# The last batch's low-rank step moved one slot earlier and done over four PSUM banks

## The chip, the cores and the metric

The kernel runs on one core of one Trainium2 chip. The metric is the device time of one execution in microseconds; the time before is 290.36 us, the median of three runs (290.25 to 290.58). TensorE is called PE below, VectorE DVE, ScalarE ACT, GpSimd POOL, and SyncE (which here only issues DMAs) SP.

## The reference

Eight batches of linear ("cosformer") attention, with 8 heads, 576 positions and head size 64, are followed by a low-rank mix over the positions and a two-layer network over the 512 channels:

```python
q_p, k_p = phi(q), phi(k)              # relu(x)*cos, relu(x)*sin -> 128 features
kv  = einsum('bhsf,bhsd->bhfd', k_p, v)
z   = sum(k_p, axis=2)
x   = einsum('bhsf,bhfd->bhsd', q_p, kv) / (einsum('bhsf,bhf->bhs', q_p, z)[..., None] + 1e-6)
x   = x.transpose(0, 2, 1, 3).reshape(B, 576, 512)
h   = x.transpose(0, 2, 1) @ U @ V     # U: 576 x 32, V: 32 x 576
u   = x + h.transpose(0, 2, 1)
out = u + maximum(u @ w_ch1, 0) @ w_ch2   # 512 -> 2048 -> 512
```

## The kernel before, in words

The 576 positions of a batch are four blocks of 128 and a rest of 64. The rests ("tails") of two batches share one block of 128 rows, so there are four pairs of tails.

For each batch attention gives x. `A_unit` then makes A = Uᵀx (32 x 512), kept as four groups of 32 rows, one for each quarter j of the channels. `u_mm` multiplies V by A: for a position block c and a channel quarter j there is one product of 32 x 128 by 32 x 128 (line 476), 16 in all, and the four j use four different groups of 32 rows of PE and four different PSUM banks. `u_add` adds x to one bank on DVE (line 484, one instruction of 128 x 512 for each j). `u_tail` does the same for a pair of tails: eight small products (line 498), then one DVE add of 128 x 128 for each j (line 505). `utr_dma` transposes u by DMA on SP's queue (lines 522 and 528); the result uT feeds the first matmul of the network.

The program is an order written out by hand. `slots` is a list of functions that mostly issue PE work; `todo` holds what is issued right after a slot. Each engine takes its own instructions in that order. Around the change the slots alternate between two kinds, and counting `slots` in the code gives these numbers:

- Even slots 200 to 214 are `half_part`: eight products of 128 x 256 (`h_ps`, line 894) of batch 5's second matmul, then one addition on DVE ("more", line 850) or a copy on ACT.
- Odd slots 201 to 215 are the first matmul of batch 6, which is worked out for a pair of hidden blocks p with seven products of half size instead of eight. `g1_cross(b, p, i)`, i from 1 to 7, issues two matmuls of 128 x 256 (`c_ps`, line 677). `g1_join` takes the results apart: ACT copies P1, U2 and P5 (line 130), DVE adds C11, C22 and C12 (line 612), ReLUs R22, R21 (ACT, line 689) and one on DVE after C12 (line 699).

For a p the crosses write three places, X and Y in one bank (`g0` or `g1`, by p's parity) and Z in bank `T`. Cross 5 opens Z and cross 3 adds to it; Z is free again when C12 has read it. Cross 4 adds to X, which C22 must have read before.

| slot | what it issues before the change |
|---|---|
| 200 | h_ps; first sum for batch 5 (`hid_sum`, line 836) |
| 201 | cross 6 of p=4, U2; then `A_unit(7)` |
| 202 | h_ps; second sum |
| 203 | crosses 1, 2 of p=5 with P1, C11; cross 5 of p=4 with P5; cross 7 of p=4 with C22, R22; then `u_mm` of j = 0, 1, 2 and `u_add` 0 |
| 204 | h_ps, more; `u_add` 1; transposing DMA of the first half of u; fourth sum |
| 205 | crosses 3, 4 of p=4 with R21, C12; cross 6 of p=5; third sum |
| 206 | h_ps; then `u_mm` of j = 3 |
| 207 | as 203, for p=6 and p=5; then `u_add` 2 |
| 208 | h_ps; `u_add` 3; transposing DMA of the second half |
| 209 | as 205, for p=5 and p=6; a weight sum (`w1_sum`, line 612) |
| 210 | h_ps, more; `u_tail` of j = 0, 1, 2 |
| 211 | as 203, for p=7 and p=6 |
| 212 | h_ps, more; `u_tail` of j = 3; transposing DMA of the tails |
| 213 | as 205, for p=6 and p=7 |
| 214 to 217 | the rest of p=7, a tail block, and four sums of batch 7's uT (`uT_sum`, line 612) |

`u_mm` and `u_tail` take PSUM through `four_banks`: the two banks of X (the tag `"X"`, another thing than the cross's X) and then what is passed in: `("s", 1)` is bank `g2`, and `T1` is bank `T`, the one that holds Z. A bank is handed on when all that read its old content have ended.

The lines that the change touches or its steps name are 440 to 507 (`A_unit`, `four_banks`, `u_mm`, `u_add`, `u_tail`), 519 to 528 (`utr_dma`), 650 to 710 (crosses and joins), and 1051 to 1083 in `attention_plan`; batch 7 has w = 187 and a_at = 14.

Of the kernel before, what the change touches and what calls it, by code (L numbers as in the profile page):

```python
# [17 lines left out]
def kernel(  # L18
# [13 lines left out]
    B = 8  # L32
# [14 lines left out]
    def tail(b):  # L47
        lo = TS * (b % 2)
        return slice(lo, lo + TS)
# [390 lines left out]
    def A_of(b):  # L440
        return A_sb[b % 4]
# [27 lines left out]
    def u_mm(b, *spare, js=range(4)):  # L469
        if b not in u_bf:  # L470
            u_bf[b] = pool.tile([P, 4, 4, P], BF16, tag="u_bf", bufs=3, name="u_bf")
        va.setdefault(b, {}).update(zip(js, four_banks(*spare)))
        for c in range(4):
            for j in js:
                rows = slice(j * R, j * R + R)
                nc.tensor.matmul(  # L476
                    out=va[b][j][:, c * P : c * P + P], lhsT=V_bf[rows, c, :],
                    rhs=A_of(b)[rows, :], start=(c == 0), stop=(c == 3),
                    tile_position=(j * R, 0),
                )  # L480
# [5 lines left out]
            in1=va[b][j].rearrange("p (c n) -> p c n", c=4), op=ALU.add,  # L486
        )

    def u_tail(pr, *spare, js=range(4)):
        if pr not in u_tl:  # L490
            u_tl[pr] = pool.tile(
                [P, DM], BF16, tag="k_p" if pr == 3 else "u_tl", bufs=1, name="u_tl"
            )
        vt = dict(zip(js, four_banks(*spare)))
        for i in range(2):
            for j in js:
                rows = slice(j * R, j * R + R)
                nc.tensor.matmul(
                    out=vt[j][tail(i), 0:P], lhsT=V_tl[rows, :],
                    rhs=A_of(2 * pr + i)[rows, :], start=True, stop=True,  # L500
                    tile_position=(j * R, i * TS),
                )
        for j in js:
            ns = slice(j * P, j * P + P)
            nc.vector.tensor_tensor(
                out=u_tl[pr][:, ns], in0=x_tl[:, ns], in1=vt[j][:, 0:P], op=ALU.add
            )
# [144 lines left out]
    def g1_cross(b, p, i):  # L652

        if (b, p) not in cross:
            if b not in hid:
                hid[b] = pool.tile([P, NJ, 512], BF16, tag="hid", bufs=2, name="hid")
            of_x, of_z = CROSS[p % 2] if b == B - 1 else (("g0", "g1")[p % 2], "T")
            xy = psum.tile([P, 512], FP32, tag=of_x, bufs=1, name="c_ps")  # L660
            cross[b, p] = {"X": xy[:, 0:256], "Y": xy[:, 256:512], "of_z": of_z}
        w = cross[b, p]
        if i == 5:
            z = psum.tile([P, 512], FP32, tag=w["of_z"], bufs=1, name="c_ps")
            w["Z"] = z[:, 0:256]
        cs = slice(p * P, p * P + P)
        to, lhs, rhs, first = {
            1: lambda: ("X", W1[0], uT_quarter(b, 0, 0), True),
            2: lambda: ("Y", W1[1], uT_quarter(b, 1, 0), False),
            3: lambda: ("Z", w1_s[4], uT_quarter(b, 1, 1), False),  # L670
            4: lambda: ("X", W1[3], uT_s[b, 4], False),
            5: lambda: ("Z", w1_s[1], uT_s[b, 1], True),
            6: lambda: ("X", w1_s[2], uT_s[b, 2], False),
            7: lambda: ("X", w1_s[3], uT_s[b, 3], False),
        }[i]()
        for d in range(2):
            nc.tensor.matmul(  # L677
                out=w[to].rearrange("p (c t) -> p c t", c=2), lhsT=lhs[:, d, cs],
                rhs=rhs[:, d], start=(first and d == 0), stop=(d == 1),
                skip_group_check=not first,  # L680
            )
# [325 lines left out]
    def attention_plan(b):  # L1007

        plan = []
        if b < 4:  # L1010
            w, f_at, q_eng, k_eng, qtr, lo = PLAN[b]
        else:
            w, q_at, k_at, qtr, lo = PLAN[b]

        def put(at, f, *a, tag=False):
            if tag:
                a = a + spare(w + at)
            plan.append((w + at, lambda: f(b, *a)))

        for n, c in enumerate(QORD):  # L1020
            if b > 3:
                put(q_at[0] + q_at[1] * n, q_prep, c, q_at[2:])
                put(k_at[0] + k_at[1] * n, k_prep, c, k_at[2:])
                put(k_at[0] + (3 * n) // 2, v_prep, 0, H, (c,), (G_,))
                continue
            if b == 3:
                q_eng, k_eng = V_ if n == 3 else A_, A_ if n < 3 else None
                put((-15, -14, -13, -2, -6)[n], q_prep, c, (q_eng, q_eng))
                put(n - 12 if n < 3 else -8, k_prep, c, (A_, k_eng))
                if n > 2:  # L1030
                    put(-4, k_prep, c, (None, V_))
                put((-9, -9, -9, -7, -5)[n], v_prep, 0, H, (c,), (A_ if n > 2 else G_,))
                continue
            put(f_at + ((n - 1) % 5 if b == 2 else n), q_prep, c, (q_eng, q_eng))
            put(f_at + 6 + n, k_prep, c, (k_eng, k_eng))
            put((-5, -2, -1, -5, -5)[n], v_prep, 0, H, (c,), (V_ if n > 2 else A_,))
        for n, (c0, c1) in enumerate(((4, 5), (0, 2), (2, 4))):
            at = qtr[n] if b > 4 else -2 if b == 3 and n == 2 else qtr + 2 * n
            put(at, qtr_dma, c0, c1)
        plan.append((w + (b == 2), lambda: kv_unit(b, 0, *spare(w), A_)))  # L1040
        plan.append((w + 2, lambda: kv_unit(b, 1, *(T1 if b == 3 else spare(w + 2)), A_)))
        for n, c in enumerate(ORD):
            if b > 3:
                put((3 if b == B - 1 else 4) + 2 * n, x_unit, c, "X", 1)
            else:
                at = 4 + n if b == 3 else 4 + (3 * n) // 2
                if n % 2:
                    put(at, x_two, c, tag=True)
                else:
                    put(at, x_unit, c, "X", 1)  # L1050
        a_at = (12, 10)[b - 2] if b < 4 else 14
        if b == B - 1:
            put(a_at, A_unit, "s", 1, A_)
        else:
            put(a_at, A_unit, tag=True)
        odd = b % 2 == 1


        def two(at):
            return [T1, ("s", 1) if at >= 86 else G3] if at >= 86 or at < 64 else [spare(at)] * 2  # L1060

        if b == B - 1:
            plan.append((w + a_at + 2, lambda: u_mm(b, ("s", 1), js=(0, 1, 2))))
            plan.append((w + a_at + 5, lambda: u_mm(b, js=(3,))))
        else:
            u_at = w + a_at + (1 if b == 3 else 2)
            plan.append((u_at, lambda: u_mm(b, *two(u_at))))
        for j in range(4):
            n = (j + 1) // 2 if b == 2 else j // 2 - 1 if b == 3 else j + (2 if b > 4 and j > 1 else 0)
            put(a_at + 2 + n, u_add, j)  # L1070
        put(a_at + (2 if b == 3 else 3), utr_dma, 0, 2)
        put(a_at + (7 if b > 4 else 3 if b == 3 else 5), utr_dma, 2, 4)
        if odd:
            if b == B - 1:
                plan.append((w + a_at + 9, lambda: u_tail(b // 2, ("s", 1), js=(0, 1, 2))))
                plan.append((w + a_at + 11, lambda: u_tail(b // 2, js=(3,))))
            else:
                at = w + a_at + (10 if b == 5 else 8 if b == 3 else 9)
                plan.append((at, lambda at=at: u_tail(b // 2, *two(at))))
            put(a_at + (11 if b > 4 else 9 if b == 3 else 10), utr_dma, 4, 5)  # L1080
        for at, t in zip(lo, loads(b + 1) if lo else ()):
            plan.append((w + at, t))
        return plan
# [44 lines left out]
    T1 = ("T", 1)  # L1128
# [221 lines left out]
    def put(at, thunk):  # L1350
        todo.setdefault(at, []).append(thunk)
# [66 lines left out]
    b6, b7 = B - 2, B - 1  # L1418
# [11 lines left out]
    def fifth(b, p):  # L1430
        g1_cross(b, p, 5)
        g1_join(b, p, "P5")

    def third(b, p):
        g1_cross(b, p, 7)
        g1_join(b, p, "C22")
        g1_join(b, p, "R22")

    def closed(b, p):
        g1_cross(b, p, 3)  # L1440
        g1_cross(b, p, 4)
        g1_join(b, p, "R21")
        g1_join(b, p, "C12")

    def crossed(*steps):
        def go():
            for f, b, p in steps:
                f(b, p)

        return go  # L1450
# [19 lines left out]
    units = [g1(b6, j) for p in range(3) for j in (p, p + 8)] + [g1(b6, 3)]  # L1470
    units.append(lambda: [opened(b6, 4), g1_main(b6, 11)])
    units.append(crossed((sixth, b6, 4)))
    for p in range(5, 8):
        units.append(crossed((opened, b6, p), (fifth, b6, p - 1), (third, b6, p - 1)))
        units.append(crossed((closed, b6, p - 1), (sixth, b6, p)))
    units.append(crossed((fifth, b6, 7), (third, b6, 7)))
    slots += units[0:2]
# [128 lines left out]
```

## Time and profile before

| | |
|---|---|
| median of the runs | 290.36 us (290.25 to 290.58) |
| the profiled execution's own time | 290.29 us |
| its span from first to last instruction | 288.5 us |
| busy: PE | 281.9 us, 98% |
| busy: DVE | 212.0 us, 73% |
| busy: ACT | 169.2 us, 59% |
| busy: POOL | 64.7 us, 22% |
| mean granted PE clock | 0.999 |
| DMA | 56.17 MB |

The span is the part that the trace covers; 1.8 us of the execution lie around it. The chain that ended last is followed back from the last instruction to what released each step. Matmuls are pipelined: one of 128 x 256 is shown as 0.27 us long, but the next starts 0.109 us later. So PE's time is read from starts, and the same holds in part for DVE and ACT. In a timeline row the columns are the start, the length of the run of equal instructions, engine, line, operation, output and inputs, shapes and count; brackets give the engine's idle time before it and what ended it.

### The profile page before, as it was taken

How to read it: one execution, taken by the hardware profiler on the slowest of the kernel's cores; microseconds unless marked ns; L12 is line 12 of the kernel's file. 1: busy time of each engine (PE TensorE's matmuls, PEld its weight loads, DVE VectorE, ACT ScalarE, POOL GpSimd, SP SyncE). 2: the span in 40 equal slices, each digit the busy share in tenths (PEclk: the TensorE clock that was granted, in tenths of full speed). 3: DMA queues.
4: the chain of work that ended last, by engine and by line, in shares of the span. 5: the costliest groups of instructions: out<-in, count | busy, mean ns of one | idle time of the engine just before them, and what ended most of it. 6: DMA issues, size and time to landing. Idle time of an engine off the chain costs nothing.

```text
span 288.5 us, 7416 instructions
## 1 busy us (share of the span) xinstructions
PE 281.9 (98%) x2961; PEld 199.0 (69%) x2992; DVE 212.0 (73%) x515; ACT 169.2 (59%) x347; POOL 64.7 (22%) x98
## 2 busy tenths in 40 slices
PE   8999999999999999999999999999999999999995
PEld 4785564446788546776766666766777889889884
DVE  5977858896876888557547794669968787775763
ACT  2955752177893557577735964497644556657310
POOL 6520500000046103302400501024201313303330
PEclk9999999999999999999999999999999999999999
DMA  7999999999999999998699939993930754436113
GB/s 225 306 254 250 278 160 192 225 328 220 363 252 202 272 248 256 203 332 207 175 227 268 245 74 250 180 339 91 183 77 9 140 120 82 88 96 112 39 75 143
DMA packets 92933, 56.17 MB, mean 195 GB/s; under 512 B 56580, under 2 KB 89732, under 8 KB 92900
## 3 DMA queue, kind: packets, MB, share of 16 engines
q1 hardware_dynamic: 82020, 43.41, 60.5%
q0 software_dynamic: 10688, 12.09, 20.7%
q8 instruction: 23, 0.38, 0.5%
q10 hardware_dynamic: 192, 0.20, 0.2%
q14 instruction: 10, 0.08, 0.1%
HBM read 36.86 MB, written 9.44 MB: 160 GB/s over the span
## 4 chain that ended last, share of the span: by engine, by line
PE 85%; DMA 8%; DVE 2%; ACT 2%; issue 1%; DVEq 0%; ACTq 0%
PE h_ps L894 32%; PE g_ps L580 26%; PE c_ps L677 7%; DMA kst<-in_k_dram 6%; PE o_ps L762 6%; PE gt_ps L722 5%; PE kv_ps L348 3%; PE x_ps L423 3%; DMA qst<-in_q_dram 2%; PE h_ps L762 1%; PE a_ps L446 1%; PE va_ps L476 1%; DVE k_p L309 1%; ACT q_p L307 1%; DVE v_ext L132 1%
## 5 line engine op out<-in xcount | busy, mean ns | idle before, releaser
L580 PE MATMUL g_ps<-uT,w_bf 128*128 128x512 bf16 x378 | 95.5, 379 | 1.1
L589 ACT ACTIVATE hid<-g_ps 128x512 bf16<-128x512 f32 x104 | 61.4, 597 | 59.7 <-PE g_ps L580 57.2
L580 PEld LDWEIGHTS <-w_bf 128*128 128x128 bf16 x402 | 37.5, 98 | 33.7
L894 PEld LDWEIGHTS <-hid 128*128 128x128 bf16 x560 | 53.0, 98 | 10.7
L894 PE MATMUL h_ps<-w_bf,hid 128*128 128x256 bf16 x336 | 43.1, 273 | 0.1
L894 PE MATMUL h_ps<-w_s,S 128*128 128x256 bf16 x240 | 30.4, 273 | 0.0
L894 PE MATMUL h_ps<-w_s,hid 128*128 128x256 bf16 x224 | 29.0, 273 | 0.0
L850 DVE TENSOR_TENSOR o_sb<-o_sb,h_ps 128x256 f32<-128x256 f32 (+1 forms) x38 | 16.9, 446 | 13.7 <-PE h_ps L894 11.2
L953 POOL DMA_DIRECT2D out_dram<-o_sb x20 | 12.9, 646 | 60.8 <-DVE o_sb L850 48.3
L894 PEld LDWEIGHTS <-S 128*128 128x128 bf16 x240 | 23.1, 98 | 4.9
L850 DVE TENSOR_TENSOR o_sb<-u_bf,h_ps 128x256 f32<-128x256 bf16 x32 | 13.3, 416 | 14.8 <-PE h_ps L894 14.6
L132 POOL CAST v_ext<-vst 128x512 bf16<-128x512 f32 (+1 forms) x22 | 16.0, 755 | 33.1 <-DMA vst<-in_v_dram 29.8
L484 DVE TENSOR_TENSOR u_bf<-x_bf,va_ps 128x512 bf16<-128x512 bf16 x27 | 17.6, 680 | 5.2 <-PE va_ps L476 4.1
L612 DVE TENSOR_TENSOR hid<-kept,c_ps 128x256 bf16<-128x256 f32 x36 | 14.7, 417 | 8.3 <-ACT kept L130 4.6
L952 POOL DMA_DIRECT2D o_sb<-u_bf x8 | 10.4, 1301 | 32.4 <-DVE rec L414 15.5
L130 ACT ACTIVATE kept<-c_ps 128x256 f32<-128x256 f32 x36 | 12.6, 384 | 7.2 <-PE c_ps L677 7.2
L722 PE MATMUL gt_ps<-uT_tl,w_bf 128*128 128x128 bf16 x256 | 16.2, 219 | 0.0
L433 DVE TENSOR_TENSOR x_bf<-x_ps,rec 128x512 bf16<-128x512 f32 x22 | 15.2, 692 | 0.8
L722 PEld LDWEIGHTS <-w_bf 128*128 128x128 bf16 x256 | 15.1, 98 | 0.7
L762 PE MATMUL o_ps<-w_bf,hid 128*128 128x512 bf16 x61 | 14.6, 379 | 0.3 <-issue 0.2
L130 ACT ACTIVATE o_sb<-h_ps 128x256 f32<-128x256 f32 x24 | 9.2, 381 | 9.4 <-PE h_ps L894 8.7
L307 ACT ACTIVATE k_p<-kst,cosw 128x512 bf16<-128x512 f32 x20 | 14.2, 713 | 0.1
(189 smaller groups left out, 459.5 us busy)
## 6 DMA issues: line engine op xcount, KB each, us to landing
qst<-in_q_dram SPq DMA_DIRECT2D x14, 512.0 KB, 5.8
kst<-in_k_dram SPq DMA_DIRECT2D x12, 512.0 KB, 7.4
out_dram<-o_sb POOLq DMA_DIRECT2D x21, 256.0 KB, 3.8
vst<-in_v_dram SPq DMA_DIRECT2D x10, 512.0 KB, 8.0
w_bf<-in_moe_w_ch_dram POOLq DMA_DIRECT2D x7, 512.0 KB, 13.3
out_dram<-o_sb SPq DMA_DIRECT2D x14, 256.0 KB, 2.4
kst<-in_k_dram SPq DMA_DIRECT2D x4, 640.0 KB, 7.0
o_sb<-u_bf POOLq DMA_DIRECT2D x8, 256.0 KB, 3.8
```

Of the source, the lines that this page charges most:

```text
L130: nc.scalar.activation(out=o, in_=i, func=AF.Copy, bias=0.0, scale=1.0)
L132: eng.tensor_copy(out=o, in_=i)
L307: nc.scalar.activation(out=o, in_=i, func=AF.Relu, bias=0.0, scale=w)
L433: nc.vector.tensor_tensor(out=x_of(b, c, rows).rearrange("p (g i d) -> p g i d", g=2, d=D), in0=view[:, :, :, 0:D], in1=rec[rows].unsqueez ...
L484: nc.vector.tensor_tensor(out=u_bf[b][:, j, :, :], in0=x_bf[b][:, :, ns], in1=va[b][j].rearrange("p (c n) -> p c n", c=4), op=ALU.add,)
L580: nc.tensor.matmul(out=g_ps.rearrange("p (c t) -> p c t", c=4), lhsT=w1_bf[:, d, j * P : j * P + P], rhs=uT[b][:, d, :, :], start=(d == 0) ...
L589: nc.scalar.activation(out=hid[b][:, j, :], in_=g_ps, func=AF.Relu, bias=0.0, scale=1.0)
L677: nc.tensor.matmul(out=w[to].rearrange("p (c t) -> p c t", c=2), lhsT=lhs[:, d, cs], rhs=rhs[:, d], start=(first and d == 0), stop=(d == 1 ...
L722: nc.tensor.matmul(out=g_ps[:, jj, :], lhsT=w1_bf[:, d, j * P : j * P + P], rhs=uT_tl[pr][:, d, :], start=(d == 0), stop=(d == 3),)
L762: nc.tensor.matmul(out=o[:, cols], lhsT=lhs[:, j, c * P : c * P + P], rhs=w2_bf[:, j, cols], start=(j == 0), stop=(j == NJ - 1),)
L850: eng.tensor_tensor(out=o, in0=x, in1=y, op=ALU.add)
L894: nc.tensor.matmul(out=acc, lhsT=lhs[:, j, :], rhs=rhs[:, j, :], start=(j == 0 and at is not None), stop=(j == 7), skip_group_check=at is ...
```

## The change

For the last batch, `A_unit` comes a slot sooner (200 in place of 201). Its u is one `u_mm` of 16 products over four banks in slot 202, the fourth bank being T, which holds j = 0; before it was 12 products in slot 203 and 4 in slot 206. All offsets of batch 7 that follow from `a_at` move by one slot, though their lines are not edited: `u_add` 0 to 3 go from slots 203, 204, 207, 208 to 202, 203, 206, 207, and the transposing DMAs of u from 204 and 208 to 203 and 207. `u_tail` of the last pair is one step of eight products in slot 210 (before six there and two in slot 212); its third bank is T, which holds j = 2, and its adds run in the order 2, 3, 0, 1. The tails' transposing DMA stays in slot 212. In slot 203 cross 7 of p=4 is issued ahead of cross 5, which writes T.

```diff
-    def u_tail(pr, *spare, js=range(4)):
+    def u_tail(pr, *spare, js=range(4), first=0):
...
-        for j in js:
+        for j in (*js[first:], *js[:first]):
...
-        a_at = (12, 10)[b - 2] if b < 4 else 14
+        a_at = (12, 10)[b - 2] if b < 4 else 13 if b == B - 1 else 14
...
         if b == B - 1:
-            plan.append((w + a_at + 2, lambda: u_mm(b, ("s", 1), js=(0, 1, 2))))
-            plan.append((w + a_at + 5, lambda: u_mm(b, js=(3,))))
+            plan.append((w + a_at + 2, lambda: u_mm(b, T1, ("s", 1), js=(1, 2, 0, 3))))
...
             if b == B - 1:
-                plan.append((w + a_at + 9, lambda: u_tail(b // 2, ("s", 1), js=(0, 1, 2))))
-                plan.append((w + a_at + 11, lambda: u_tail(b // 2, js=(3,))))
+                plan.append((w + a_at + 10, lambda: u_tail(b // 2, T1, ("s", 1), first=2)))
...
-            put(a_at + (11 if b > 4 else 9 if b == 3 else 10), utr_dma, 4, 5)
+            put(a_at + (12 if b == B - 1 else 11 if b == 5 else 9), utr_dma, 4, 5)
...
+    def seventh_first(b, p):
+        g1_cross(b, p, 7)
+        fifth(b, p)
+        g1_join(b, p, "C22")
+        g1_join(b, p, "R22")
...
     for p in range(5, 8):
-        units.append(crossed((opened, b6, p), (fifth, b6, p - 1), (third, b6, p - 1)))
+        if p == 5:
+            units.append(crossed((opened, b6, p), (seventh_first, b6, p - 1)))
+        else:
+            units.append(crossed((opened, b6, p), (fifth, b6, p - 1), (third, b6, p - 1)))
```

## The prediction

> **What bounds the kernel now.** I read the page's sums, then the chain that ended last, then the timeline where the change lies.
>
> ```profile
> PE 281.9 (98%) x2961; PEld 199.0 (69%) x2992; DVE 212.0 (73%) x515; ACT 169.2 (59%) x347; POOL 64.7 (22%) x98
> ...
> PE 85%; DMA 8%; DVE 2%; ACT 2%; issue 1%; DVEq 0%; ACTq 0%
> ```
>
> PE bounds the whole. From 246 us to its end PE's starts have no gap over 0.02 us, and between 235 and 246 one of 0.03 us; so what PE loses or saves before 235 us arrives at the end undiminished. What the two removed steps cost PE (start, length):
>
> ```profile
> 227.22 1.04 PE L894 MATMUL h_ps<-w_s,S 128*128 128x256 bf16 x8
> ...
> 228.19 0.39 PE L476 MATMUL va_ps<-A_sb,V_bf 32*128 32x128 bf16 x4
> ...
> 228.51 0.61 PE L677 MATMUL c_ps<-uT,w_bf 128*128 128x256 bf16 x4
> ...
> 232.96 1.04 PE L894 MATMUL h_ps<-w_bf,hid 128*128 128x256 bf16 x8
> ...
> 233.93 0.24 PE L498 MATMUL va_ps<-A_sb,V_tl 32*64 32x128 bf16 x2
> ...
> 234.10 0.39 PE L677 MATMUL c_ps<-uT,w_s 128*128 128x256 bf16 x2
> ...
> 234.48 0.38 PE L677 MATMUL c_ps<-uT_s,w_bf 128*128 128x256 bf16 x2
> ```
>
> Batch 6 has a 16-product step, and shows how soon its add follows:
>
> ```profile
> 194.29 0.40 PE L476 MATMUL va_ps<-A_sb,V_bf 32*128 32x128 bf16 x16
> 194.62 1.05 PE L894 MATMUL h_ps<-w_bf,hid 128*128 128x256 bf16 x8
> 194.72 0.69 DVE L484 TENSOR_TENSOR u_bf<-x_bf,va_ps 128x512 bf16<-128x512 bf16 x1 [0.77 <-PE va_ps L476]
> ```
>
> Last, DVE alone in the same stretch:
>
> ```profile
> 223.01 0.69 DVE L836 TENSOR_TENSOR S<-S,hid 128x1024 bf16<-128x1024 bf16 x1
> 225.43 0.75 DVE L612 TENSOR_TENSOR hid<-kept,c_ps 128x256 bf16<-128x256 f32 x2 [1.73 <-ACT kept L130]
> 226.10 0.68 DVE L484 TENSOR_TENSOR u_bf<-x_bf,va_ps 128x512 bf16<-128x512 bf16 x1
> ...
> 229.63 0.75 DVE L612 TENSOR_TENSOR hid<-kept,c_ps 128x256 bf16<-128x256 f32 x2
> 230.30 1.28 DVE L484 TENSOR_TENSOR u_bf<-x_bf,va_ps 128x512 bf16<-128x512 bf16 x2
> 231.50 0.41 DVE L612 TENSOR_TENSOR hid<-kept,c_ps 128x256 bf16<-128x256 f32 x1
> ...
> 233.09 0.68 DVE L505 TENSOR_TENSOR u_tl<-x_tl,va_ps 128x128 bf16<-128x128 bf16 x3
> 233.68 0.75 DVE L612 TENSOR_TENSOR hid<-kept,c_ps 128x256 bf16<-128x256 f32 x2
> ```
>
> From 225.43 to 235.95 us DVE has no idle row: it is the second limit here. In this stretch it runs up to a slot and more behind PE, and the order of its queue decides when PSUM places are free again.
>
> **What PE saves.** Eight h_ps at 0.109 us after 227.22 end at 228.09, and the next cross starts at 228.51: the four-product step costs 0.42 us (its products run one after another, and the switch of shape costs 0.10 ahead and about 0.09 behind). The two-product tail step costs 234.10 - 233.83 = 0.27 us. Sixteen products cost no more than twelve: 194.62 - 194.29 = 0.33 from the first product to the next h_ps, as for the twelve, 225.35 to 225.68; for eight tail products against six I take the same 0.27, with 0.03 as upper bound of the difference (two products 3 to 4 ns apart). One wait goes: cross 4 of p=6 in slot 213 starts its pair 0.15 us late because C22 ends at 234.43. Together 0.84 us. A one slot sooner costs nothing: its 20 products take 0.49 us in either place, x of the last block is ready at 222.05 against 222.88 now, and the copy of A on ACT (0.51 us behind the first product, 0.28 long) ends at 223.67, 0.79 us ahead of its use. If that cover were gone, PE would wait by what is lacking.
>
> **What it now waits for.** I walk the three queues from slot 200 (h_ps at 221.91, the same in both) with the rows' spacings: cross pair on PE 0.22; DVE 0.335 for a C join, 0.60 for `u_add` and for a sum, 0.45 and 0.21 for C12 and its ReLU, 0.20 for a tail add; 0.05 from an end to the waiting engine. The same walk over the kernel before gives h_ps of slot 214 at 234.83; the trace has 234.92.
>
> 1. Slot 202: the u step starts at 224.46, PE goes on at 224.79, `u_add` 0 runs 224.89 to 225.57. Crosses 1, 2 of p=5 and cross 7 of p=4 last until 225.44; cross 5 writes T, which `u_add` 0 still reads, and waits until 225.62: +0.17 us. Behind it P5's copy ends at 226.43 and C22 starts at 226.47; DVE, which stands in order, is idle from 225.97 to 226.47. So of its 1.73 us idle before, now 1.2 + 0.5 remain: the head start is lost. Behind C22 wait `u_add` 1, more, the fourth sum and C12: C12 of p=4 starts at 228.34, before 228.30.
> 2. Slot 207: cross 5 of p=5 would start at 228.67, and T is free of C12 at 228.80: +0.13.
> 3. `u_add` 2 is issued in slot 206, now ahead of C11 and C22 of slot 207. The third sum runs at 229.0, `u_add` 2 at 229.6, C11 at 230.2, C22 until 230.94 (before 230.38). Cross 4 of p=5 could start at 230.32 and waits until 230.99: +0.67, the largest term.
> 4. Slot 210: the four-bank tail step finds T free (C12 ends at 231.88, the step comes at 232.3). But the first tail add stands behind `u_add` 3, C12 and its ReLU, the weight sum and more, and runs 233.06 to 233.34. Cross 5 of p=6 could start at 233.0 and waits until 233.39: +0.39.
>
> Together 1.36 us. Slot 214 then starts at 235.35: +0.52 against the walk of before, +0.43 against its trace. ACT's queue: R22 of p=5 waits for C22 until 230.98, and the h_ps copy and R21 behind it end at 231.95, before their next users (c1 of p=7 at 232.57). POOL's stores move with "more" and are followed by nothing that PE reads. SP's queue holds only the three transposing DMAs: the first goes at 227.6 (before 227.85), the second as before at 231.6, landing at 234.3 for a sum at 237.0; the tails' at 234.0 (before 234.99) for a matmul at 261.6. All hidden; a landing 2.7 us later would stop DVE.
>
> Prices that the trace doesn't show: each of the four waits has as lower end nothing (DVE is early) and as upper end one further `u_add` in front, 0.60. Waits 1 and 4 share a bank that the old step never held. I take the walked values, which reproduce the old order within 0.09 us, rounded up to +0.55, since a wait that I left out can only add. A difference of about 0.2% (0.58 us) is what a measurement of this kernel can tell from none.
>
> **The rivals.**
> *DVE's head start holds (faster).* If C22 of p=4 isn't late, DVE keeps the 0.5 us: wait 2 and 4 vanish, wait 3 shrinks to 0.17, and 0.84 saved minus 0.34 gives 289.86; without wait 3 too, 289.69. It decides where cross 5 of p=4 finds T free by 225.44. For it: DVE's 1.73 us of idle time ahead of 225.43. Against it: the add starts 0.43 us behind its first product and lasts 0.68, so T isn't free before 225.6.
> *The gain on PE is not passed on (no change).* DVE's list of work is the same, so its last join of this stretch could come when it did and PE meet it there: 290.4. The Trainium skill (TensorEngine Tiling (Array Packing), section PSUM Bottleneck) says that tiling makes TensorE faster but not the emptying of PSUM, which may become the bottleneck; by that rule alone the merged steps would gain nothing. The trace agrees as to DVE's unbroken 10.5 us. Against no change: C22 of p=5 is moved behind one more add of 0.60.
> *The delay builds up (much slower).* If one more `u_add` gets ahead of a join, or the tail adds end behind C11 of p=7, PE pays 0.60 once more: about 291.4. For it: DVE has no idle time until 235.95 to catch up. Against it: PE being late gives DVE time, and from 236.7 on it idles again.
>
> **How the numbers follow.** The sum stands against the profiled execution, 290.29 us, 0.07 below the median of 290.36; forecasts are from the median. Likeliest, 0.66: the four waits outweigh the saving, +0.3 to +0.8, at 290.36 + 0.55 = 290.9 us; the bound of 290.94 lies in its middle, so 0.32 of it is "same" and 0.34 "slower". No change: 0.12. Much slower: 0.14. Head start holds: 0.08, of which 0.06 beyond 0.2%. So faster 0.06, same 0.32 + 0.12 + 0.02 = 0.46, slower 0.48. The range runs from the low side of no change, 290.1, to the built-up delay, 291.4; it leaves out the head start and some of the last.
>
> **What would show it.** In the new trace: one L476 step of 16 products near 224.5 and one L498 step of 8; no gap of four products at 228; `u_add` 0 starting near 224.9, inside DVE's old idle time; C22 of p=4 after an idle DVE near 226.5; gaps in PE's starts ahead of c_ps of about 0.17, 0.13, 0.67 and 0.39 us near 225.6, 228.8, 231.0 and 233.4; slot 214's h_ps near 235.4. The prediction is wrong if the L612 pair of slot 207 starts before 229.7 or if cross 4 of p=5 doesn't wait.

## The result and the profile after

| | before | after |
|---|---|---|
| median, eight executions each | 290.38 us (290.22 to 290.92) | 291.73 us (290.71 to 292.28) |
| the profiled execution | 290.29 us, span 288.5 | 291.97 us, span 290.1 |

The ratio is 1.0038, with a 95% interval of 1.0022 to 1.0055: slower by about 0.4%, clear of noise, and the median 0.3 us above the end of the forecast range.

The spans differ by 1.6 us, and the trace divides them. A stage is read from PE's starts: the first h_ps of slot 200, the first h_ps of slot 214, and the last matmul.

| | start of slot 200 | slot 200 to slot 214 | slot 214 to the last matmul |
|---|---|---|---|
| before | 221.91 | 13.00 | 49.82 |
| after | 223.10 | 13.46 | 49.82 |
| difference | +1.19 | +0.46 | 0.00 |

So 0.46 us arise in the slots that the change touches, and 1.19 us arise ahead of them, in work that the change does not touch. Nothing is given back later.

The changed slots first. PE's timeline after, from the 16-product step to the last wait ahead of slot 214 (start, length of the run, then the instruction):

```profile
225.66 0.40 PE L476 MATMUL va_ps<-A_sb,V_bf 32*128 32x128 bf16 x16
...
226.44 0.79 PE L677 MATMUL c_ps<-uT_s,w_s 128*128 128x256 bf16 x4
...
229.47 0.60 PE L677 MATMUL c_ps<-uT,w_bf 128*128 128x256 bf16 x4
230.02 0.60 PE L677 MATMUL c_ps<-uT_s,w_s 128*128 128x256 bf16 x4
...
231.32 0.38 PE L677 MATMUL c_ps<-uT,w_s 128*128 128x256 bf16 x2
232.21 0.38 PE L677 MATMUL c_ps<-uT_s,w_bf 128*128 128x256 bf16 x2 [0.50 <-DVE hid L612]
...
233.61 0.26 PE L498 MATMUL va_ps<-A_sb,V_tl 32*64 32x128 bf16 x8
233.80 0.61 PE L677 MATMUL c_ps<-uT,w_bf 128*128 128x256 bf16 x4
234.59 0.60 PE L677 MATMUL c_ps<-uT_s,w_s 128*128 128x256 bf16 x4 [0.18 <-DVE u_tl L505]
```

Two crosses in a row (four matmuls) take 0.44 us to the next start, one takes 0.22, so each wait can be read off. The run at 226.44 is 0.79 long where such runs are 0.60: 0.19 us of wait lie inside it, ahead of cross 5 of p=4. The run after 229.47 could have started at 229.91 and starts at 230.02: 0.11, ahead of cross 5 of p=5. The pair after 231.32 could have started at 231.54 and starts at 232.21: 0.67, ended by a join. The last could have started at 234.24 and starts at 234.59: 0.35, ended by a tail add. The brackets name shorter idle times because a matmul is shown as 0.27 us long while PE could take the next after 0.109.

DVE's timeline after, in the same stretch:

```profile
226.11 0.69 DVE L484 TENSOR_TENSOR u_bf<-x_bf,va_ps 128x512 bf16<-128x512 bf16 x1 [1.22 <-PE va_ps L476]
227.06 0.42 DVE L612 TENSOR_TENSOR hid<-kept,c_ps 128x256 bf16<-128x256 f32 x1 [0.27 <-ACT kept L130]
227.68 0.42 DVE L612 TENSOR_TENSOR hid<-kept,c_ps 128x256 bf16<-128x256 f32 x1 [0.20 <-ACT kept L130]
...
229.55 0.41 DVE L612 TENSOR_TENSOR hid<-kept,c_ps 128x256 bf16<-128x256 f32 x1
...
230.81 0.68 DVE L484 TENSOR_TENSOR u_bf<-x_bf,va_ps 128x512 bf16<-128x512 bf16 x1
231.41 0.74 DVE L612 TENSOR_TENSOR hid<-kept,c_ps 128x256 bf16<-128x256 f32 x2
...
234.26 0.87 DVE L505 TENSOR_TENSOR u_tl<-x_tl,va_ps 128x128 bf16<-128x128 bf16 x4
```

The add starts 0.45 us behind the first product. The two joins behind it each wait for a copy on ACT, so DVE idles again. The first two waits end 0.05 us after a reader of T: `u_add` 0, which ends at 226.80, and C12 of p=4, the row at 229.55, which ends at 229.96. `u_add` 2 at 230.81 now stands ahead of the joins at 231.41, and the tail adds come at the end of an unbroken row.

Now the 1.19 us ahead of slot 200. This is DVE's first use of q, in the kernel before, the changed kernel, and the kernel before submitted once more:

```profile
6.96 1.67 DVE L309 TENSOR_SCALAR q_p<-qst,cosw 128x512 bf16<-128x512 f32 x4 [2.15 <-DMA qst<-in_q_dram]
```

```profile
7.80 1.67 DVE L309 TENSOR_SCALAR q_p<-qst,cosw 128x512 bf16<-128x512 f32 x4 [2.98 <-DMA qst<-in_q_dram]
```

```profile
8.05 1.67 DVE L309 TENSOR_SCALAR q_p<-qst,cosw 128x512 bf16<-128x512 f32 x4 [3.23 <-DMA qst<-in_q_dram]
```

In the changed kernel's profile DVE waited 0.84 us longer for the first q, and 1.09 us longer when the unchanged kernel was profiled again. The rest of the 1.19 us was lost at 29 us: batch 1's q had landed at 25.23 instead of 23.62 us, DVE came to it later, and PE's transposes of it waited for DVE's copies.

The loads were not all that came late. Ahead of its transposes of q PE runs a row of matmuls on zeros (line 235). In the kernel before these went from 0.43 us apart to 0.22 at about 5 us, in the changed kernel's profile at about 7, and PE's first transpose of q came at 8.88 us instead of 7.90. A later profile parts the two: in the version called "all three" below, q was used slightly earlier than in the kernel before, and PE was late all the same. Its two rows, and PE's row of the kernel before:

```profile
6.91 1.68 DVE L309 TENSOR_SCALAR q_p<-qst,cosw 128x512 bf16<-128x512 f32 x4 [2.10 <-DMA qst<-in_q_dram]
```

```profile
8.89 1.95 PE L378 MATMUL t_ps<-ident,q_p 128*128 128x128 bf16 x32
```

```profile
7.90 2.11 PE L378 MATMUL t_ps<-ident,q_p 128*128 128x128 bf16 x32
```

At the first matmul of line 894 (78.73 against 78.14 us) that version was still 0.59 us behind, with batch 1's q early too (DVE came to it at 23.38 us, before at 23.65). In the changed kernel's profile both the loads and PE's pace were late; what each alone would have cost there is not shown.

### The profile page after: what moved, and what is told of

It reads as the page before. It is cut to its first block, busy times and chain, and to the rows that moved or that the text cites. A ratio compares the mean times of both kernels' runs of the same rounds, so it can differ in the third digit from the quotient of the medians.

```text
span 290.1 us, 7415 instructions
## 1 busy us (share of the span) xinstructions
PE 282.6 (97%) x2961; PEld 199.1 (69%) x2992; DVE 213.2 (73%) x515; ACT 169.6 (58%) x347; POOL 64.4 (22%) x98
## 4 chain that ended last, share of the span: by engine, by line
PE 84%; DMA 7%; DVE 5%; ACT 2%; issue 1%; DVEq 0%; ACTq 0%
PE h_ps L894 31%; PE g_ps L580 26%; DMA qst<-in_q_dram 7%; PE c_ps L677 6%; PE o_ps L762 6%; PE gt_ps L722 5%; PE kv_ps L348 3%; PE x_ps L423 3%; PE h_ps L762 1%; DVE q_p L309 1%; PE a_ps L446 1%; PE va_ps L476 1%; ACT q_p L307 1%; DVE v_ext L132 1%; DVE u_bf L484 0%
## 5 line engine op out<-in xcount | busy, mean ns | idle before, releaser
L953 POOL DMA_DIRECT2D out_dram<-o_sb x20 | 12.9, 646 | 62.4 <-DVE o_sb L850 47.7
L132 POOL CAST v_ext<-vst 128x512 bf16<-128x512 f32 (+1 forms) x22 | 14.9, 707 | 34.4 <-DMA vst<-in_v_dram 31.8
```

The source lines that it names most:

```text
L132: eng.tensor_copy(out=o, in_=i)
```

## The experiments

Each run has one profile, and the stage from slot 200 to slot 214 is the measure, since it has the same length whenever the loads land. All runs end in the same 49.82 us behind slot 214.

**Both kernels again.** No edit.

> The changed kernel once more, unedited. Theory A (the change costs what its queues cost, and the rest of the measured difference is a late start that comes and goes): from the first h_ps matmul of slot 200 to that of slot 214 13.45 us as in its first profile (kernel before: 13.01), and a time that falls in two groups, about 290.8 us (290.36 + 0.45) when the first loads land as in the kernel before, and about 291.9 when they land late. Theory B (the new program as such starts later): every execution lies above 291.4, and batch 1's k lands after 29 us in the profile (kernel before: 28.1).

> The kernel before once more, unedited, as a control of what a new submission alone does to the start. Theory A: also here an execution may start late and then lies about 1.2 us above 290.4; most lie at 290.2 to 290.6. Theory B: none lies above 291.

The changed kernel's stage took 13.45 us, the kernel before 13.00, as in the first profiles. Slot 200 started at 222.72 in the changed kernel and at 223.09 in the kernel before, which is as late as the changed kernel's first profile. The whole times no longer show two narrow groups: the changed kernel had a median of 291.70 us (290.96 to 293.37, 12 executions), the kernel before beside it 291.23 (290.11 to 293.15, 35 executions); ratio 1.0028, interval 1.0009 to 1.0046. The kernel before against itself gave 1.0003 (0.9978 to 1.0028). Theory B, that the new program as such starts later, falls as it was put: the changed kernel's executions begin at 290.96, its second profile has batch 1's k landing at 28.30 us, and the old program starts as late at times (k landing at 29.49 in its second profile); 35 executions of it spread over 3 us where the first eight had spread over 0.7. Whether the new program starts later on average is another question, left open below. The part of theory A that expected two groups of times falls too.

A second place where loads count showed up in these profiles. ACT's timeline of the kernel with u merged alone (next experiment), around 77 us:

```profile
76.87 0.72 ACT L307 ACTIVATE q_p<-qst,cosw 128x512 bf16<-128x512 f32 x1 [0.74 <-DMA qst<-in_q_dram]
...
81.79 0.36 ACT L130 ACTIVATE s_sb<-h_ps 128x256 f32<-128x256 f32 x1
```

Batch 2's q landed late there. ACT stood 0.74 us, and the copy out of PSUM behind it in ACT's queue, at 81.79, came later too; in the kernel before that copy ran at 81.00. PE lost 0.6 us to it at 82.2. The changed kernel's second profile lost its last 0.6 us at the same place.

**Each merged step alone.** First u in one step, the tails in two as before:

```diff
-                plan.append((w + a_at + 10, lambda: u_tail(b // 2, T1, ("s", 1), first=2)))
+                plan.append((w + a_at + 10, lambda: u_tail(b // 2, ("s", 1), js=(0, 1, 2))))
+                plan.append((w + a_at + 12, lambda: u_tail(b // 2, js=(3,))))
```

> The change without its last part: A in slot 200 and u in one step of 16 products with T as fourth bank, the tails in two steps as before. If the queue order on DVE is the cause, walking the queues gives +0.3 to +0.4 us against the kernel before from slot 200 to slot 214 (13.3 to 13.4 us): the waits of cross 5 for u_add 0 (0.17) and of cross 4 of p=5 for C22 (0.67) stay, the one of cross 5 of p=6 behind the tail add goes. If the two merged steps cost independently, each has half of the 0.45, about +0.2.

Then, in the kernel before, only the tails in one step (and the parameter `first`):

```diff
-                plan.append((w + a_at + 9, lambda: u_tail(b // 2, ("s", 1), js=(0, 1, 2))))
-                plan.append((w + a_at + 11, lambda: u_tail(b // 2, js=(3,))))
+                plan.append((w + a_at + 9, lambda: u_tail(b // 2, T1, ("s", 1), first=2)))
```

> The kernel before with only the last pair's tails in one step over four banks in slot 210 (T holds j = 2, adds in the order 2, 3, 0, 1). The walk gives +0.4 to +0.5 us from slot 200 to slot 214 (13.4 to 13.5 us): no wait at slot 209, but cross 5 of p=6 waits about 0.9 us for T behind the first tail add, and 0.42 us of saving is lost with it. If the two merged steps cost independently: about +0.2 us, with a wait of 0.35.

The stage took 13.38 us with u alone and 13.47 with the tails alone: +0.38 and +0.47, and both together +0.45. They don't add up, so they are not two independent costs. In whole times u alone came out at 1.0027 of the kernel before (1.0003 to 1.0052), the tails alone at 1.0023 (1.0004 to 1.0043). With u alone the waits were 0.19, 0.12 and 0.66 us. With the tails alone the main one is this, in PE's timeline:

```profile
232.64 0.61 PE L677 MATMUL c_ps<-uT,w_bf 128*128 128x256 bf16 x4
233.91 0.60 PE L677 MATMUL c_ps<-uT_s,w_s 128*128 128x256 bf16 x4 [0.66 <-DVE u_tl L505]
```

233.91 - 232.64 - 0.44 is a wait of 0.83 us for the first tail add to free bank T. Another 0.07 us lie inside the tail step (eight products in 0.33 us, where the changed kernel has 0.26): the third product, the first on T, waits for C12 to leave it. So PE saved 0.27 us and a wait of 0.15, and stood 0.90: +0.48, and the stage shows +0.47. The expectation had 0.9 for the wait, all of it in one place.

**The joins ahead of the adds.** `u_add` 2 and 3 back behind the joins of slot 207:

```diff
-            put(a_at + 2 + n, u_add, j)
+            put(a_at + 2 + n + (b == B - 1 and j > 1), u_add, j)
...
-        put(a_at + (7 if b > 4 else 3 if b == 3 else 5), utr_dma, 2, 4)
+        put(a_at + (8 if b == B - 1 else 7 if b > 4 else 3 if b == 3 else 5), utr_dma, 2, 4)
```

> The changed kernel with u_add 2 and 3 put back behind the joins, in slots 207 and 208 (and the second half's transposing DMA in 208). If each wait were a cost of its own, the wait of cross 4 of p=5 for C22 (0.66 us) would go and slot 200 to slot 214 would take about 12.9 us. If DVE's amount of work up to the first tail add sets the pace, the wait only moves: 0.1 ahead of cross 4 and of the tail step each, and about 0.85 ahead of cross 5 of p=6, so 13.45 to 13.5 us, no gain.

The stage took 13.46 us: no gain, though the largest wait nearly went. PE's timeline:

```profile
230.56 0.38 PE L677 MATMUL c_ps<-uT,w_s 128*128 128x256 bf16 x2
230.84 0.38 PE L677 MATMUL c_ps<-uT_s,w_bf 128*128 128x256 bf16 x2
...
232.56 0.61 PE L677 MATMUL c_ps<-uT,w_bf 128*128 128x256 bf16 x4
233.83 0.60 PE L677 MATMUL c_ps<-uT_s,w_s 128*128 128x256 bf16 x4 [0.66 <-DVE u_tl L505]
```

The wait for C22 is down from 0.67 to 0.06 us, and the one for the first tail add is up from 0.35 to 0.83; 0.12 more lie inside the tail step, for T. DVE reached that add after the same list of work, so PE met it at the same time. The expectation of a wait as a cost of its own (12.9 us) falls.

**DVE's lost head start.** `u_add` 1 in slot 202, right behind `u_add` 0:

```diff
-            put(a_at + 2 + n, u_add, j)
+            put(a_at + 2 + n - (b == B - 1 and j == 1), u_add, j)
```

> The changed kernel with u_add 1 issued in slot 202 right behind u_add 0, so that it fills the idle 0.5 us of DVE between C11 of p=5 and C22 of p=4. If that idle time is what loses DVE's head start, the walk gives 13.0 us from slot 200 to slot 214 (0.45 to 0.5 less than the changed kernel), with waits of 0.17, 0, 0.3 and 0.4. If the order alone counts (an add more in front of C11 and C22), it is worse than 13.45.

The stage took 12.98 us, 0.47 less than the changed kernel. DVE's timeline shows what the edit does: the two joins run back to back now, behind two adds, and the idle rows ahead of them are gone.

```profile
226.21 1.28 DVE L484 TENSOR_TENSOR u_bf<-x_bf,va_ps 128x512 bf16<-128x512 bf16 x2 [1.22 <-PE va_ps L476]
227.41 0.79 DVE L612 TENSOR_TENSOR hid<-kept,c_ps 128x256 bf16<-128x256 f32 x2
```

That is the whole loss of the changed kernel won back by moving one instruction of 0.68 us. The waits left are 0.19, 0, 0.30 and 0.35 us, together the 0.84 that PE saves. This version, the one before it and the next one have one execution each (291.57, 291.17 and 290.60 us), so only their stages count.

**The weight sum in the idle time.** The 0.68 us sum of slot 209 goes to slot 202:

```diff
-        (1, 1, -8), (2, 1, -6), (3, 1, -4), (1, 0, -3), (4, 1, -2), (3, 0, -1), (2, 0, 11), (4, 0, 23),
+        (1, 1, -8), (2, 1, -6), (3, 1, -4), (1, 0, -3), (4, 1, -2), (3, 0, -1), (2, 0, 11), (4, 0, 16),
```

> The changed kernel with the weight sum of slot 209 (0.68 us on DVE) moved to slot 202, into DVE's idle time ahead of u_add 0. The walk: only the wait of cross 5 of p=6 shrinks, 0.35 to about 0.15, the 0.66 stays: 13.2 to 13.25 us from slot 200 to slot 214. If DVE's order doesn't matter there: 13.45.

13.30 us: the wait for the tail add shrank from 0.35 to 0.20 us, the 0.66 stayed. The gain is 0.15 us where about 0.2 was expected, for a reason that DVE's timeline shows:

```profile
231.94 0.29 DVE L699 TENSOR_SCALAR hid<-hid 128x512 bf16<-128x512 bf16 x1
232.59 0.42 DVE L850 TENSOR_TENSOR o_sb<-o_sb,h_ps 128x256 f32<-128x256 f32 x1 [0.36 <-PE h_ps L894]
```

With the weight sum out of the way DVE stands 0.36 us for slot 210's h_ps, which the wait of 0.66 us has made late. From the ReLU's start to that of the addition it is 0.65 us, against 0.81 in the changed kernel with the sum between them, so only 0.16 of the 0.60 us that the sum takes in the queue are won. In the next version, where the wait of 0.66 is gone, this idle time is gone as well.

**All three.** The two edits of `u_add` and the one of the weight sum together.

> The changed kernel with all three: u_add 1 in slot 202, u_add 2 and 3 behind the joins, the weight sum in slot 202. The walk leaves two waits of 0.17 us (cross 5 of p=4 for u_add 0, cross 5 of p=6 for the first tail add) and gives 12.5 us from slot 200 to slot 214: 0.5 less than the kernel before (13.0) and 0.95 less than the changed one. If it is PSUM bank T as such that makes the merged steps dear, not DVE's order, it stays above 13.0.

> The version with the three moved DVE instructions again. Slot 200 to slot 214: 12.63 us, so 0.37 less than the kernel before and 0.82 less than the changed one; its median should lie about 0.4 us below that of the kernel before and 0.8 below that of the changed one measured beside it, if the late loads strike all alike.

The stage took 12.63 us both times: 0.37 less than the kernel before and 0.82 less than the changed one. The walk had said 12.5. PE's timeline of the first of them:

```profile
226.04 0.78 PE L677 MATMUL c_ps<-uT_s,w_s 128*128 128x256 bf16 x4
...
230.81 0.38 PE L677 MATMUL c_ps<-uT,w_s 128*128 128x256 bf16 x2
231.03 0.38 PE L677 MATMUL c_ps<-uT_s,w_bf 128*128 128x256 bf16 x2
...
232.43 0.33 PE L498 MATMUL va_ps<-A_sb,V_tl 32*64 32x128 bf16 x8
232.69 0.61 PE L677 MATMUL c_ps<-uT,w_bf 128*128 128x256 bf16 x4
233.36 0.60 PE L677 MATMUL c_ps<-uT_s,w_s 128*128 128x256 bf16 x4
```

The waits ahead of slot 207's cross and for C22 (231.03 - 230.81 is the plain 0.22) are gone. The two for bank T remain, 0.18 (0.78 against 0.60) and 0.23 (233.36 - 232.69 - 0.44), and a third, which the walk did not have, lies inside the tail step: 0.07 (0.33 against 0.26), for C12 to leave T. So the waits for bank T still cost 0.48 us, and the 0.84 us of saving on PE outweigh them once DVE keeps up: 0.36, where the stage shows 0.37. In whole times this version came out at 0.9995 of the kernel before (0.9976 to 1.0014) and then at 0.9985 (0.996 to 1.001), with medians of 290.77 against 290.94 and 290.70 against 291.20 us; 0.37 us is a ratio of 0.9987, which the second matches but neither can tell from no change. The second median lies 0.50 us below that of the kernel before, where 0.4 was expected, and 1.32 below that of the changed kernel beside it (next experiment), where 0.8 was. By the stage it beats both kernels, by the whole time only the changed one.

**The changed kernel a third time.**

> The changed kernel a third time, to compare whole times next to the other two. Slot 200 to slot 214: 13.45 us. If the late loads strike all programs alike, its median lies 0.45 us above that of the kernel before measured beside it, whatever both are; if the changed program itself starts later, more than 1 us above.

The stage was 13.45 us again, and slot 200 started at 223.35. The median was 292.02 us against 291.20 for the kernel before beside it, a difference of 0.82; ratio 1.0031, interval 1.0006 to 1.0055. That lies between the two expectations. 0.45 us would be a ratio of 1.0016, which is inside this interval and the second one but below the first (from 1.0022).

## Why the prediction was right and wrong

**The walk of the queues was right, term by term.** The four waits, forecast as 0.17, 0.13, 0.67 and 0.39 us, were 0.19, 0.11, 0.67 and 0.35: 1.32 us against 1.36. They stand where they were put and were ended by what was named, and neither sign of being wrong came. One place differs: the walk has C11 of p=5 right behind `u_add` 0 and DVE idle for 0.5 us ahead of C22, where the trace has 0.27 us ahead of C11 and 0.20 ahead of C22. The wait of 0.15 us in slot 213 went, the 16 products took no longer than the 12 (0.33 us to the next PE work), and A a slot sooner cost nothing. The sum was +0.43 to +0.52, taken as +0.55; the stage shows +0.45 in each of three profiles (13.45 or 13.46). The rounding up, "since a wait that I left out can only add", was not earned: nothing had been left out.

**The mechanism held.** DVE's order and amount of work set the pace. Merging either step alone lost about as much as both. Taking away the largest wait moved it to the next place. Filling the idle time that the late copies of P1 and P5 leave on DVE won everything back.

**The rivals.** That DVE's head start holds was wrong for the changed kernel. Its condition was that T be free in time for cross 5 of p=4, and T came 0.19 us late. But with `u_add` 1 moved T came as late and the loss was gone, and C11, which doesn't wait for T, has 0.27 of the 0.47 us of idle time; so T is not what decides. Nor did that version reach this rival's 0.5 us of gain: wait 3 only fell to 0.30, wait 4 stayed at 0.35, and the stage came out even (12.98 against 13.00). That the gain is not passed on had the right engine: DVE's work up to the tail adds decides. But PE did not come out even, since DVE also lost its head start, and PE lost 0.45 us. The Trainium skill (TensorEngine Tiling (Array Packing), section PSUM Bottleneck) says that emptying PSUM may become the bottleneck when tiling speeds PE up; the trace agrees, with 1.32 us of waits against 0.84 saved, and goes beyond it, since by that rule alone nothing would have been lost. That the delay builds up did not come: the stage behind slot 214 kept its 49.82 us.

**What failed is the base and the range.** The step was "The sum stands against the profiled execution, 290.29 us, 0.07 below the median of 290.36", and with it that 0.58 us is what a measurement tells from none. It takes the start of the execution as fixed: the sum has no term for when the loads land and when PE reaches its pace. Nothing ahead of the prediction showed that this moves, since the three times lay within 0.33 us. The later runs showed it. Over more executions the kernel before itself runs from 290.0 to 293.4 us, and its median in the later comparisons is 290.9 to 291.2, above the slowest of its eight executions in the result (290.92); the changed kernel's stays at 291.7 to 292.0. Of the 1.35 us between the two medians of the result, 0.46 come from the changed slots and the rest from the start, as the two profiles divide theirs (0.46 and 1.19). The range of 290.1 to 291.4 was made from the terms of the change alone; it lacks the start's 1.2 us on its upper side.

**What stays open.** In its three profiles the changed kernel starts slot 200 at 223.10, 222.72 and 223.35; the kernel before at 221.91 and 223.09; the seven profiles of versions with parts of the change or edits to it between 221.92 and 223.20. The instructions ahead of slot 200 are the same in all. The three whole-time ratios of the changed kernel, 1.0038, 1.0028 and 1.0031, are 0.8 to 1.1 us, about twice what its stage explains, while the version with all three edits shows none that is clear of noise. Whether the changed program starts later on average, by some tenths of a microsecond, or whether it was unlucky, these runs do not settle. The later comparisons ran on three chips (numbers 15, 8 and 1), and which one ran the first is not on record; whether the chip matters was not tried. Nor was it tried why DVE's first use of q comes between 0.2 us earlier and 1.1 us later, or what the order of crosses 7 and 5 in slot 203, which is part of the change, does alone.

## What to carry to other kernels

Where a second engine works without a gap beside the bound one, a PE saving is worth what that engine's queue lets through: list its instructions in order to the place where PE meets it, and look for idle time to move work into before moving PE's work. A wait that vanishes is only a gain if the next meeting point also comes earlier. And time a stage inside the trace when whole executions scatter by more than the change: here the stage repeats within 0.01 us, while whole executions spread over 3.

## What was not expected of the hardware

The identical kernel's time depends on how it starts: DVE's first use of q came at 6.96 us in one profile and at 8.05 in another of the same program, and slot 200, 215 us later, still stood 1.18 us behind.

PE's clock followed a rhythm of its own at the start. In the kernel before, the matmuls of 128 x 512 on zeros went from 0.43 us apart to 0.22 at about 5 us; in the changed kernel's profile they did so at about 7 us, with the same instructions ahead of them. The trace's record of the full granted clock begins at 4.89 us in the one and at 6.88 in the other, and anywhere from 4.07 to 6.90 us in the twelve profiles. A late clock alone can cost time: in the version with all three edits it came at 6.90 us, and 0.59 us of delay remained though q was early.
